# Weights fetched in pairs of blocks, and one partition a unit for the block numbers, in a sparse attention with a channel mix

## The chip, the core and the metric

The kernel runs on one core of a Trainium2 chip. The metric is the device time of one execution in microseconds (us), the median of several. TensorE (PE in the rows) does the matmuls, with its weight loads shown as PEld; VectorE is DVE, ScalarE ACT, GpSimd POOL, and SyncE (SP) issues every DMA transfer of this kernel.

## The reference

Block-sparse attention over 4 sequences of 768 positions, 8 heads of 64, in blocks of 32; then a channel mix on its output, with shifted input, a gate and a squared ReLU.

```python
scores = 0.125 * q @ k.T                      # (4, 8, 768, 768)
mask = |blk_i - blk_j| <= 1 or blk_i, blk_j in (0, 23)
for qb in range(24):                          # three sampled blocks a row of blocks
    for kb in sampled_blocks[qb]:
        mask[qb, kb] = True
x = softmax(where(mask, scores, -1e9)) @ v    # (4, 768, 512)

x_prev = x shifted by one position
xk = mu_k * x + (1 - mu_k) * x_prev
xr = mu_r * x + (1 - mu_r) * x_prev
kk = relu(xk @ w_k) ** 2                      # 512 -> 1024
out = sigmoid(xr @ w_r) * (kk @ w_v)          # 1024 -> 512
```

The three weights w_r (512 x 512), w_k (512 x 1024) and w_v (1024 x 512) arrive as 64-bit floats, everything else as 32-bit floats or integers. The sampled blocks are an input, known only when the kernel runs.

## The kernel before

**Attention** goes by 26 units. A near unit (22 of them, one for each row of blocks n = 1 to 22) takes row n of all four sequences at once: 128 query rows against eight blocks of keys: 0, 23, n-1, n, n+1 and the three sampled ones. Four wide units do rows 0 and 23 of one sequence against all keys. A unit runs through scores (TensorE, line 584), maximum (VectorE, 594), exponentials (ScalarE, 557 or 631), a turn so that the keys lie on partitions (for the first three units by TensorE and a copy, 547 to 553; later by VectorE's transpose, 635, and four transfers, 643), values (TensorE, 617 or 655), division (VectorE, 737 to 748), and a turn of the result into channels by positions (776 and 793, or 757 to 766). Keys go to `KA`, values to `VA`. The neighbours lie in rings of places that the units share; the sampled blocks are fetched by transfers whose source is a register (506 and 523). `keys_again` copies a block that stands in two places.

**The registers** come from `packed`: for each near unit one integer of six 5-bit block numbers (three for keys, and three for values, where a block that is already in the window gets the number of an empty block). `mask_setup` fetches the sampled numbers with the seven numbers that each is compared to (`drawn`, line 334) and packs them by nine VectorE instructions on one partition, 22 units side by side. SP then loads one register a unit (439).

**The weights** are 20 blocks of 128 x 512: four of w_r, eight of w_k, eight of w_v. Each arrives as raw 64-bit words, 0.5 MB in one transfer (425), and is turned into a 32-bit float by a magnitude (ScalarE, 381), a tail (VectorE, 388), a sign (VectorE, 391, or ScalarE, 400, by the set `SIGN_ACT`) and a join (VectorE, 394), and then into two parts that TensorE multiplies fast: the high part (GpSimd, 410, or ScalarE, 412, by `HI_POOL`) and what is left (415; VectorE or GpSimd by `LO_DVE`). The two parts are written to the place of the raw words, which have the same tag `w{i}` and one buffer. The intermediate tiles have three buffers a tag (`zr`, `kk`).

**The channel mix** goes by 12 tiles of 256 positions, tile 1 first and tiles 0 and 11 last: split input (845 to 857), gate for each half (881), hidden part in four pairs of 128 channels (899), values (928), each matmul three times over the parts.

**The order** of all this is made when the kernel is built. Every operation is added to a `Plan` with its engine, a duration, what it reads and writes, and a rank (roughly the time at which it is wanted, lower first), to which a table `SHIFT` adds a number by the operation's position in the list. `Plan.order` runs through time: on each engine, among the operations that could start within `NEAR` ns of the earliest one, it takes that of the lowest rank. A transfer needs one of `FLIGHT` = 8 places in flight, a group of three gathers needs three. It also models that TensorE's instructions come in chunks (`CHUNK` instructions, at least `FETCHED` ns from one to the next). The instructions are then written out in that order, so every engine does its own list strictly in turn, and SP too: a transfer that waits holds up those behind it. The constants (`PICK`, `UNIT_AT`, `RAW_AT`, `WEIGHT_AT`, `SHIFT` and others) stand in the file as numbers.

## Time and profile before

| | |
|---|---|
| median of 3 runs | 536.41 us (532.74, 536.41, 538.78) |
| the profiled execution | 536.71 us |
| its span, first to last instruction | 534.9 us |
| mean granted clock of TensorE | 0.993 of full speed |
| busy: PE, DVE, ACT, POOL | 484.0, 284.9, 327.2, 206.6 us |
| moved by DMA | 115.68 MB, 216 GB/s on the mean |

The profile shows one execution, and its durations are from that one. Busy times are sums over an engine's instructions; issuing transfers doesn't count. A row gives a start in us, a duration, the engine, the line, the operation, out<-in with shapes, a count, and in brackets how long the engine had stood idle and what ended that.

### The profile page before, as it was taken

How to read it: one execution, taken by the hardware profiler on the slowest of the kernel's cores; microseconds unless marked ns; L12 is line 12 of the kernel's file. 1: busy time of each engine (PE TensorE's matmuls, PEld its weight loads, DVE VectorE, ACT ScalarE, POOL GpSimd, SP SyncE). 2: the span in 40 equal slices, each digit the busy share in tenths (PEclk: the TensorE clock that was granted, in tenths of full speed). 3: DMA queues.
4: the chain of work that ended last, by engine and by line, in shares of the span. 5: the costliest groups of instructions: out<-in, count | busy, mean ns of one | idle time of the engine just before them, and what ended most of it. 6: DMA issues, size and time to landing. Idle time of an engine off the chain costs nothing.

```text
span 534.9 us, 17726 instructions
## 1 busy us (share of the span) xinstructions
PE 484.0 (90%) x7260; PEld 394.7 (74%) x7260; DVE 284.9 (53%) x573; ACT 327.2 (61%) x744; POOL 206.6 (39%) x198
## 2 busy tenths in 40 slices
PE   0077699999999999999989999999999999999997
PEld 0034469778768878777967877978877888889896
DVE  2889786765565565465555566375555352223201
ACT  2489986865675676655676566663684662646340
POOL 2354236422612531532621441632351633628270
PEclk9979999999999999999999999999999999999999
DMA  8999988898888888788978897999748433010001
GB/s 303 399 402 326 339 258 245 276 266 263 231 243 257 246 254 245 209 234 225 249 234 255 242 252 235 305 283 335 217 111 290 112 85 81 21 40 1 21 21 39
DMA packets 58628, 115.68 MB, mean 216 GB/s; under 512 B 7730, under 2 KB 20786, under 8 KB 55603
## 3 DMA queue, kind: packets, MB, share of 16 engines
q1 hardware_dynamic: 58546, 114.55, 70.3%
q8 instruction: 57, 0.93, 0.8%
q14 instruction: 25, 0.20, 0.1%
HBM read 77.82 MB, written 6.29 MB: 157 GB/s over the span
## 4 chain that ended last, share of the span: by engine, by line
PE 59%; DMA 16%; SPq 11%; ACT 6%; DVE 4%; issue 4%; POOL 0%; ACTq 0%; DVEq 0%
PE v L928 17%; PE h_3p L899 6%; DMA pt<-r 6%; PE h_0p L899 5%; PE h_2p L899 5%; PE h_1p L899 5%; PE r_1p L881 4%; PE r_0p L881 4%; PE o L655 4%; SPq L643 3%; PE s L584 3%; DMA raw<-w_v 3%; DMA xm<-rx 3%; PE o L719 2%; PE sw L677 2%
## 5 line engine op out<-in xcount | busy, mean ns | idle before, releaser
L928 PE MATMUL v<-w,k 128*128 128x512 f32 (+1 forms) x600 | 143.4, 390 | 0.9 <-ACT h_3k L912 0.9
L928 PEld LDWEIGHTS v<-w,k 128*128 128x128 f32 x600 | 107.2, 188 | 28.8 <-issue 4.9
L584 PE MATMUL s<-KA,q 64*32 64x256 f32 x1408 | 48.5, 399 | 29.4 <-DMA raw<-w_v 25.8
L631 ACT ACTIVATE p<-s,nm 128x256 f32<-128x256 f32 x152 | 63.1, 480 | 8.5 <-DVE r L635 8.3
L635 DVE STREAM_TRANSPOSE r<-p 128x1024 f32<-128x1024 f32 x38 | 45.9, 1228 | 27.1 <-DMA pt<-r 25.9
L584 PEld LDWEIGHTS s<-KA,q 64*32 64x32 f32 x1408 | 25.7, 110 | 44.5 <-issue 34.8
L594 DVE TENSOR_REDUCE nm<-s 128x4 f32<-128x1024 f32 x44 | 53.0, 1213 | 9.6 <-PE s L584 9.3
L655 PEld LDWEIGHTS o<-VA,pt 128*32 128x32 f32 x2432 | 37.1, 109 | 14.7 <-issue 8.2
L655 PE MATMUL o<-VA,pt 128*32 128x65 f32 x2432 | 42.3, 221 | 6.2 <-DMA pt<-r 3.1
L857 POOL TENSOR_TENSOR xr<-xr_0f,xr 128x256 fp32r<-128x256 f32 x24 | 18.4, 765 | 76.2 <-ACT xr L855 67.4
L857 POOL TENSOR_TENSOR xr<-xr_1f,xr 128x256 fp32r<-128x256 f32 x24 | 17.8, 744 | 76.5 <-ACT xr L855 73.8
L899 PEld LDWEIGHTS h_0p<-xk,w 128*128 128x128 f32 x288 | 35.8, 191 | 3.1 <-ACT z L888 1.7
L899 PE MATMUL h_0p<-xk,w 128*128 128x256 f32 x288 | 37.3, 284 | 0.9 <-ACT z L888 0.7
L899 PE MATMUL h_3p<-xk,w 128*128 128x256 f32 x288 | 38.0, 285 | 0.0
L748 DVE TENSOR_TENSOR x<-o,R 128x128 f32<-128x128 f32 x96 | 23.9, 317 | 25.7 <-ACT xt L766 13.6
L899 PEld LDWEIGHTS h_2p<-xk,w 128*128 128x128 f32 x288 | 35.9, 191 | 2.2 <-ACT k L913 0.4
L899 PE MATMUL h_2p<-xk,w 128*128 128x256 f32 x288 | 37.4, 284 | 0.0
L899 PE MATMUL h_1p<-xk,w 128*128 128x256 f32 x288 | 37.2, 284 | 0.0
L899 PEld LDWEIGHTS h_3p<-xk,w 128*128 128x128 f32 x288 | 36.0, 191 | 1.6 <-ACT k L913 0.6
L899 PEld LDWEIGHTS h_1p<-xk,w 128*128 128x128 f32 x288 | 35.6, 191 | 1.3 <-ACT xr_1d L845 0.4
L881 PE MATMUL r_1p<-w,xr 128*128 128x512 f32 x144 | 36.4, 397 | 0.0
L881 PE MATMUL r_0p<-w,xr 128*128 128x512 f32 x144 | 36.4, 397 | 0.0
(139 smaller groups left out, 795.5 us busy)
## 6 DMA issues: line engine op xcount, KB each, us to landing
VA<-vt SPq DMA_DIRECT2D x92, 260.0 KB, 4.2
KA<-kt SPq DMA_DIRECT2D x89, 256.0 KB, 4.4
pt<-r SPq DMA_DIRECT2D x76, 256.0 KB, 5.0
VA<-vw SPq DMA_DIRECT2D x24, 260.0 KB, 4.6
KA<-kq SPq DMA_DIRECT2D x16, 384.0 KB, 5.4
ptw<-rw SPq DMA_DIRECT2D x32, 192.0 KB, 3.9
out<-z SPq DMA_DIRECT2D x23, 256.0 KB, 4.4
q<-qt SPq DMA_DIRECT2D x22, 256.0 KB, 4.7
```

The source lines that it names most:

```text
L584: nc.tensor.matmul(s.ap[ROWS[j], row, a * 256 : (a + 1) * 256].rearrange("p (n x) -> p n x", x=BLK), q.ap[half, (hp * QB + j) * BLK : (hp ...
L594: nc.vector.tensor_reduce(out=nm.ap.rearrange("p (r a) -> p r a", r=2), in_=s.ap.rearrange("p r (a x) -> p r a x", a=2), axis=AX.X, op=ALU ...
L631: plan.add(ACT, 365, t1 + O_EXP[kind], lambda row=row, a=a, i=i: nc.scalar.activation(p.ap[:, :, :, i, :].rearrange("p j c x -> p c j x"), ...
L635: plan.add(DVE, N_TURN, t1 + O_TURN[0], lambda: nc.vector.transpose(out=r.ap[:, :, gi].rearrange("p j c i x -> p j (c i x)"), in_=p.ap.rea ...
L643: nc.sync.dma_start(pt.ap[:, b].rearrange("p g c i x -> p (g c i x)"), r.ap[ROWS[b]].rearrange("p j g c i x -> p j (g c i x)"))
L655: nc.tensor.matmul(o[gi].ap[ROWS[j], i * DV : (i + 1) * DV], pt.ap[:, j, gi, g, 2 * row + a, :], VA.ap[:, c0 + g, j, h * DV : (h + 1) * DV ...
L677: nc.tensor.matmul(s.ap[HALF[a], row, 0:W], q.ap[half, 2 * hp * BLK : 2 * (hp + 1) * BLK], wide_keys(b, hp)[half, k * W : (k + 1) * W], st ...
L748: nc.vector.tensor_tensor(out=to[:, :, 2 * e : 2 * e + 2], in0=o[i].ap.rearrange("p (c e v) -> p c e v", e=2, v=DV)[:, :, e, 0:D].rearrang ...
L857: plan.add(POOL, 160 + 2.17 * MIX * tw, rank + O_MIX, lambda f=f, cs=cs: nc.gpsimd.tensor_tensor(out=dst.ap[:, 1, cs], in0=f.ap, in1=dst.a ...
L881: nc.tensor.matmul(pr.ap[:, 0:512], xr.ap[:, a, c, :], weight_of["r", c].ap[:, w, :], start=(c == 0 and m == 0), stop=(c == CC - 1 and m = ...
L899: nc.tensor.matmul(ph.ap[:, ff * TT : (ff + 1) * TT], weight_of["k", c, f2 // 2].ap[:, w, f % 4 * P : (f % 4 + 1) * P], xk.ap[:, a, c, :], ...
L928: nc.tensor.matmul(pv.ap[:, 0:width], k2.ap[:, a, f, i * P : (i + 1) * P], weight_of["v", f].ap[:, w, cs], start=(f == 0 and m == 0), stop ...
```

## The change

Raw weights come two blocks at a time: ten transfers of 1 MB into tiles of two blocks, whose place then holds the four parts of both blocks. The transfer counts as one write of both halves, and a place is given back as a whole: a tile of parts can be written when the raw tile in the same place has been read for both blocks. The numbers of the sampled blocks lie on 22 partitions, one for each near unit, and are packed there; the register of unit n is loaded from partition n-1. The two mixing vectors come in one transfer, and their complement is made by one instruction. The sets that choose engines for parts and copies, the constants of the order's model and the whole table of ranks are others; what is computed is the same.

```diff
-    CHUNK, FIRST, FETCHED, FLIGHT = 258, 214, 6200, 8
+    CHUNK, FIRST, FETCHED, FLIGHT = 254.05, 186.0, 4600, 8
...
-    packed = fixed([1, NEARS], I32, "packed")
+    packed = fixed([NEARS, 1], I32, "packed")
...
-        drawn = buf([1, 2, pairs, 2], I32, "x0", 1, "drawn")
-        e = buf([1, NEARS, NRAND, SAME_AS], F32, "x1", 1, "equal")
-        r = buf([1, 6, NEARS, NRAND], F32, "kk", 3, "pickf")
+        drawn = buf([NEARS, 2, NRAND * SAME_AS, 2], I32, "x0", 1, "drawn")
+        e = buf([NEARS, NRAND, SAME_AS], F32, "x1", 1, "equal")
+        r = buf([NEARS, 6, NRAND], F32, "kk", 3, "pickf")
...
-        for w, m in enumerate((mu_k, mu_r)):
-            plan.add(SP, ISSUE, 20, lambda w=w, m=m: nc.sync.dma_start(mk.ap[:, w, :], m), writes=[(mk, w)], size=20000)
-            plan.add(DVE, 150, 25, lambda w=w: nc.vector.tensor_scalar(
-                out=mk.ap[:, 2 + w, :], in0=mk.ap[:, w, :], scalar1=-1.0, scalar2=1.0, op0=ALU.mult, op1=ALU.add),
-                reads=[(mk, w)], writes=[(mk, 2 + w)])
+        plan.add(SP, ISSUE, 20, lambda: nc.sync.dma_start(mk.ap[:, 0:2, :], mu), writes=[(mk, 0, 1)], size=40000)
+        plan.add(DVE, 150, 25, lambda: nc.vector.tensor_scalar(
+            out=mk.ap[:, 2:4, :], in0=mk.ap[:, 0:2, :], scalar1=-1.0, scalar2=1.0, op0=ALU.mult, op1=ALU.add),
+            reads=[(mk, 0, 1)], writes=[(mk, 2), (mk, 3)])
...
-            tile_in = raws[name]
-            raw, here = tile_in.ap, (tile_in,)
+            tile_in, half = raws[name]
+            raw, here = tile_in.ap[:, half], (tile_in, half)
...
-        w = buf([P, 2, 512], F32R, f"w{i}", 1, f"w{i}")
-        weight_of[name] = w
+        two = i // 2
+        if i % 2 == 0:
+            pairs[two] = buf([P, 2, 2, 512], F32R, f"w{two}", 1, f"w{two}")
+        whole, e = pairs[two], i % 2
+
+        weight_of[name] = (whole, e)
...
+    def two_blocks(which, c, f=0):
+        w = {"r": w_r, "k": w_k, "v": w_v}[which]
+        return w[c * P : (c + 2) * P, f * 512 : (f + 1) * 512].rearrange("(a p) x -> p a x", p=P)
...
-            for i, (name, src) in enumerate(jobs):
-                raw = raws[name] = buf([P, 512, 2], I32, f"w{i}", 1, f"raw{i}")
-                plan.add(SP, ISSUE, RAW_AT[i], lambda raw=raw, src=src: nc.sync.dma_start(raw.ap.rearrange("p x b -> p (x b)"), src.bitcast(I32)),
-                         writes=[(raw,)], release=RAW_AT[i], size=524288)
+            for i in range(0, len(jobs), 2):
+                name, src = jobs[i]
+                raw = buf([P, 2, 512, 2], I32, f"w{i // 2}", 1, f"raw{i // 2}")
+                for e in range(2):
+                    raws[jobs[i + e][0]] = (raw, e)
+                src = two_blocks(*name)
+                plan.add(SP, ISSUE, RAW_AT[i // 2], lambda raw=raw, src=src: nc.sync.dma_start(raw.ap.rearrange("p a x b -> p a (x b)"), src.bitcast(I32)),
+                         writes=[(raw, 0, 1)], release=RAW_AT[i // 2], size=1048576)
...
-            sampled[n, by] = by.value_load(packed.ap[0:1, n - 1 : n], min_val=0, max_val=ROOM ** (2 * NRAND) - 1)
+            sampled[n, by] = by.value_load(packed.ap[n - 1 : n, 0:1], min_val=0, max_val=ROOM ** (2 * NRAND) - 1)
...
-ISSUE, FETCH, FIND = 560, 760, 850
+ISSUE, FETCH, FIND = 560, 740, 380
...
-HI_POOL = frozenset([0, 1, 7, 9, 10, 16, 17, 18])
-LO_DVE = frozenset([0, 3, 5, 6, 8, 14, 16, 19])
-SIGN_ACT = frozenset([0, 3, 4, 5, 6, 8, 15, 16, 17, 19])
-TURN_DVE = frozenset(['0_1_0', '1_0_1', '1_1_0', '1_1_1', '2_1_0'])
+HI_POOL = frozenset([0, 5, 6, 7, 9, 10, 13, 14, 15, 17])
+LO_DVE = frozenset([5, 6, 8, 16, 18])
+SIGN_ACT = frozenset([0, 1, 4, 5, 6, 15, 16, 19])
+TURN_DVE = frozenset(['0_0_0', '0_0_1', '1_1_0', '1_1_1', '2_0_0', '2_1_0', '2_1_1'])
```

The ranks that SP goes by at the start, each the sum of the operation's constant and its number in `SHIFT`, lowest first, without those whose place is still in use by unit 0. In raw transfers r, k and v are the weight, the digits its row blocks, and f0 and f1 the halves of w_k's columns; q0 is unit 0's q.

| before | rank | after | rank |
|---|---|---|---|
| raw r3 | -5033.9 | drawn | -5284.4 |
| values 0 | -4932.3 | keys 23 | -5270.5 |
| raw v2 | -4912.3 | keys 0 | -4775.0 |
| raw k1 f1 | -4805.7 | raw r2, r3 | -3950.6 |
| raw k2 f0 | -4805.6 | raw v0, v1 | -2008.8 |
| keys 23 | -4769.8 | raw r0, r1 | -957.1 |
| drawn | -4769.6 | raw k2, k3 f0 | -317.2 |
| raw v1 | -4762.9 | raw v6, v7 | -11.8 |
| raw r0 | -4762.8 | q0 | -0.6 |
| values 2 | -4723.9 | keys 1, 2 | -0.3 |
| raw k3 f0 | -4715.7 | q1 | 1.2 |
| q1 | -4514.2 | values 0 | 5.4 |
| sampled keys, unit 0 | -4514.1 | raw v2, v3 | 5.7 |
| raw k1 f0 | -4411.6 | raw k0, k1 f0 | 8.0 |
| mu_k | -177.2 | values 23, unit 1 | 8.1 |
| keys 1, 2 | -175.4 | sampled keys, unit 0 | 8.9 |
| keys 0 | -175.4 | values 1 | 9.7 |
| values 1 | -175.4 | values 2 | 12.9 |
| raw v4 | -131.9 | raw v4, v5 | 19.0 |
| q0 | 11.4 | sampled values, unit 1 | 26.1 |
| raw v0 | 11.5 | values 23 | 29.5 |
| raw r1 | 11.6 | sampled keys, unit 1 | 30.0 |

## Rows read from the trace of the kernel before

**Rows 1.** The page's first line.
```profile
span 534.9 us, 17726 instructions
```
**Rows 2.** Stages (from:to, length): busy us of each engine, TensorE's clock, DMA share, GB/s.
```profile
core 0: us, PE busy (x) PEld busy (x) DVE busy (x) ACT busy (x) POOL busy (x), PEclk, DMA share, GB/s
0.00:26.00 26.00, 0.15 (x8) 0.18 (x16) 13.67 (x28) 8.41 (x13) 7.26 (x13) 1.00 0.93 348
26.00:68.00 42.00, 30.24 (x733) 19.11 (x728) 35.72 (x73) 37.50 (x83) 17.84 (x16) 0.92 0.98 356
68.00:400.00 332.00, 322.02 (x5277) 261.71 (x5276) 193.28 (x391) 217.45 (x506) 124.35 (x116) 1.00 0.85 247
```
**Rows 3.** TensorE's waits, 25 to 70 us: total us, times, longest.
```profile
PE s L584 <- DMA raw<-w_v: 25.8, 1, 25.8
PE t L547 <- ACT p L557: 3.4, 4, 1.8
```
**Rows 4.** TensorE in order of time, 25 to 110 us.
```profile
25.85 3.67 PE L584 MATMUL s<-KA,q 64*32 64x256 f32 x64 [25.85 <-DMA raw<-w_v]
...
62.44 1.67 PE L617 MATMUL o<-VA,pt 128*32 128x65 f32 x99 [0.95 <-issue]
64.41 1.09 PE L584 MATMUL s<-KA,q 64*32 64x256 f32 x28 [0.30 <-ACT nm L598]
66.72 0.62 PE L584 MATMUL s<-KA,q 64*32 64x256 f32 x4 [1.22 <-issue]
...
67.70 3.01 PE L881 MATMUL r_0p<-w,xr 128*128 128x512 f32 x12
```
**Rows 5.** SP's issues in order of time, from the start.
```profile
0.75 0.39 SPq L425 DMA_DIRECT2D raw<-w_r  x1
...
8.38 0.33 SPq L425 DMA_DIRECT2D raw<-w_k  x1
...
16.60 2.14 SPq L508 DMA_DIRECT2D KA<-kt  x3
```
**Rows 6.** Transfers issued up to 18.8 us: count, KB each, us to landing.
```profile
raw<-w_k SPq DMA_DIRECT2D x4, 512.0 KB, 7.2
raw<-w_v SPq DMA_DIRECT2D x3, 512.0 KB, 7.8
KA<-kt SPq DMA_DIRECT2D x5, 256.0 KB, 7.8
raw<-w_r SPq DMA_DIRECT2D x2, 512.0 KB
VA<-vt SPq DMA_DIRECT2D x3, 260.0 KB, 8.2
q<-qt SPq DMA_DIRECT2D x2, 256.0 KB
KA<-kt SPq DMA_DIRECT2D x1, 512.0 KB, 8.1
```
**Rows 7.** Groups by line, 26 to 68 us: busy us, mean ns | idle before.
```profile
L415 POOL TENSOR_TENSOR w<-wf,w 128x512 fp32r<-128x512 f32 x10 | 13.8, 1393 | 8.0 <-ACT w L412 7.2 <-DMA VA<-vt 0.4
L381 ACT ACTIVATE wmag<-raw 128x512 f32<-128x512 f32 x12 | 8.3, 702 | 3.1 <-DMA raw<-w_r 3.1
L388 DVE TENSOR_SCALAR wf<-raw 128x512 uint16<-128x512 uint16 x11 | 5.5, 516 | 0.0
L400 ACT ACTIVATE wf<-raw 128x512 f16<-128x512 f32 x6 | 4.7, 813 | 0.9 <-DMA raw<-w_v 0.9
L412 ACT CAST w<-wf 128x512 fp32r<-128x512 f32 x7 | 4.3, 629 | 0.3 <-DVE wf L394 0.3
```
**Rows 8.** Stages at the start, as in the second group.
```profile
0.00:13.00 13.00, 0.00 (x0) 0.00 (x0) 3.21 (x10) 2.92 (x4) 3.20 (x9) 1.00 0.84 299
13.00:27.00 14.00, 1.15 (x24) 0.76 (x32) 11.28 (x20) 5.49 (x9) 5.06 (x5) 1.00 1.03 400
```
**Rows 9.** VectorE's first packing instruction, in order of time.
```profile
10.01 0.63 DVE L341 TENSOR_TENSOR equal<-drawn 1x462 f32<-1x462 int32 x1 [4.93 <-DMA drawn<-blocks]
```
**Rows 10.** The page's list of transfers.
```profile
KA<-kt SPq DMA_DIRECT2D x89, 256.0 KB, 4.4
```

108 lines of the change are left out of this document (56 added, 52 removed).

## The prediction

> **What bounds the kernel now.** I read the cores' page first for the span, then the busy times of five stages, then what TensorE waited for, and then the start in order of time. The span is 534.9 us [rows 1]; the profiled execution took 536.71 us, so 1.8 us lie around it, and the median of the three runs is 536.41. The sum below is made against 536.7. A difference under 1% (5.4 us) is about what a measurement of this kernel cannot tell from none: its three runs alone lie 6 us apart.
>
> The stages [rows 2] tell where TensorE is not working: 25.9 us of the first 26, 11.8 of the next 42 (42 less 30.24), 10.0 of the 332 up to 400. So from about 68 us TensorE sets the pace with little to win; most of its idle time lies ahead of that. There is one long wait, 25.8 us before the first scores [rows 3]; the view names a weight transfer as its releaser, but the weights are not read by the scores. What they read is q and the keys, the sampled ones last: these were asked for from 16.60 us on, in 2.14 us [rows 5], and took 7.8 us to land [rows 6], which gives 26.5 us, near enough to the start at 25.85 [rows 4]. The first gate starts at 67.70 [rows 4] and with it the mixer, which fills TensorE. Between 26 and 68 us it is ScalarE (37.5 of 42 us) and VectorE (35.7) that are nearly full, and the DMA engines (0.98) [rows 2]. Of ScalarE's 37.5 us, 17.3 are turning raw weights into pairs of parts: 8.3 + 4.7 + 4.3 us [rows 7]. The same engines were busy for only 8.4 and 13.7 us of the first 26 [rows 2]. The start is thus a queue of transfers, and behind it a queue of conversions that stand in the way of the first three units' attention.
>
> **The change, part by part.**
>
> *Transfers.* Nine raw transfers of 0.524 MB were issued before 18.8 us, with six of keys (1.84 MB), three of values (0.80) and one q that is in time (0.26; the second was issued last): 7.62 MB up to the sampled keys [rows 6]. The engines moved 299 GB/s in the first 13 us (3.89 MB) and 400 after [rows 8], so 7.62 MB are through at 13 + 3.73/0.4 = 22.3 us; the first scores come 3.5 us behind that, which I take as the time to land and be seen. In the changed kernel I set the table of ranks in the section on the change against the rule that SP takes the lowest rank among what can start (in the trace of before its first eleven issues, from 0.75 to 8.38 us [rows 5], stand in that order, but for a value transfer whose place was being cleared). Ahead of unit 0's sampled keys then stand seven raw transfers of 1.049 MB (7.34 MB), keys 0 and 23 (0.52), keys 1 and 2 (0.52), two q (0.52), two values (0.53) and the sampled keys themselves (0.79): 10.2 MB, through at 13 + 6.3/0.4 = 28.8 us, so scores at 32.3 us, 6.5 later than now. From below this is bounded by 25.85 (the gathers could go at once when the packed words are there, as they did before), from above by two more values and the eighth raw transfer going first (1.6 MB, 3.9 us: 36.3), since a group of three gathers needs three free places in flight and may lose its turn to single transfers. I take 32.3, the ranks' own order. With larger transfers in flight the first 13 us may also fill better: between 400 and 299 GB/s there are 3.3 us, of which about 2 are the time before the first bytes. I take 1.1 us, with 0 and 1.3 as ends.
>
> *Conversions.* What lands early instead are weights. By 26 us six blocks had their magnitude made (the other lines of that instruction: twelve from 26 to 68 [rows 7], two later); by the order above about eleven have. Five blocks more move into a stretch in which ScalarE had 17.6 us free. One block costs ScalarE 0.70 us for the magnitude, 0.8 x 8/20 for the sign and 0.63 x 10/20 for the high part by the new sets: 1.33 us; five are 6.7 us [rows 7]. The new sets take two signs, two high parts and two turned copies (at some 0.6 us, as a high part) from ScalarE, 4.1 us in all, of which I count 2.5 in this stage. They go to GpSimd and VectorE: GpSimd gets two copies and three subtractions more (3 x 1.39 and less [rows 7]); it is busy 17.8 of these 42 us [rows 2], so this is covered, and if not, a weight comes some 5 us later. ScalarE then has 37.5 - 6.7 - 2.5 = 28.3 us of work, which at today's density (37.5 of 42) lasts 31.7 us. First scores at 32.3 - 1.1 = 31.2, first gate at 62.9 instead of 67.7: **4.8 us gained**, as the difference of a loss of 5.4 and a gain of 10.2.
>
> *Sharing one place by two blocks.* The high part of a pair's first block cannot be written before the raw words of both have been read: that is one magnitude, one tail and one sign more, 0.70 + 0.50 + 0.79 = 2.0 us [rows 7] on one block in two. It costs nothing where weights are early; the queue behind it is GpSimd's or ScalarE's own next copy. If the pair is the one for which the first gate waits, it costs 2.0. Between 0 and 2.0 I take 0, because with this order the gate's blocks land among the first three pairs, some 40 us ahead.
>
> *Fewer issues.* Ten raw issues and one vector's less are some 0.35 to 0.6 us each on SP, 4 to 5 us, in a stretch where SP mostly waits for places in flight. I take 0, with 1 us gained as the other end.
>
> *Packing.* The blocks' numbers landed at 10.0 us, as the wait of the first packing instruction shows [rows 9]; now they go first. Packing on 22 partitions shortens the long instructions: the first, over 462 elements, took 0.63 us [rows 9] and is now over 21. This saves 1 to 2 us of VectorE and makes the gathers ready some 7 us sooner, which by itself gives nothing while they stand behind seven weights. The mixing vectors come in one transfer and take one small instruction of VectorE less, where nobody waits for them: 0. Reading a register from another partition than the first is not in this trace: between 0 and 0.3 us each for 22 of them, off TensorE's path; I take 0.
>
> *The order anew, and its fetch model.* All of the order is worked out again with other constants. One can be read from the trace: after a gap TensorE ran 99 + 28 = 127 matmuls, each with its load (254 instructions), and stood again with no releaser until 66.72, which is 4.3 us after 62.44 [rows 4]. The changed constants say 254 instructions and 4.6 us, the old ones 258 and 6.2. An order that knows this can put such gaps where TensorE waits anyway. The gaps seen here are 0.95 and 1.22 us; I take 1.4 us gained, with 0 and 3 as ends, and for the rest of the span (10.0 us of idle time from 68 to 400) 0, between 4 lost and 4 gained.
>
> **Sum:** 536.7 - 4.8 - 1.4 = **530.5 us**. Put together the ends give 521 to 541.
>
> **Rivals.**
>
> *Scores late, chain as long (slower).* The interval from first scores to first gate was 67.70 - 25.85 = 41.85 us [rows 4]. Three units are a chain (scores, maximum, exponentials, turns, values, division, turn, mixing), and if its latency, not ScalarE's load, sets those 42 us, then the scores that come 6.5 us later push the gate to 74.2 and the time to 543.2. It decides from an interval of 35.3 us: above it the change loses, below it wins. For it speaks that TensorE's own waits in this stage are on steps of the chain (3.4 us for the exponentials [rows 3]); against it that ScalarE is 89% full there, nearly half of it with weights.
>
> *It comes out even.* Gathers are issued as soon as they can be and weights fill in as now, or the interval shrinks by about those 6.5 us only: scores 26 to 32, gate 66 to 68. 536 us, between 533 and 539. For it speaks that the same 10.5 MB of weights and the same keys must pass the DMA engines at 0.98 before the gate.
>
> *Each transfer has a fixed price.* 256 KB land in 4.4 us over the whole run [rows 10] and 512 KB in 7.2 [rows 6]; a straight line through these leaves 1.6 us at no bytes. Were that time of the DMA engines, eleven transfers less would give 17.6 us: 519 us. Against it: with 512 KB transfers the engines already ran at 1.03 busy and 400 GB/s from 13 to 27 us [rows 8], so the 1.6 us overlap with other transfers. The Trainium skill has such a rule ("DMA: Bandwidth & Descriptors", Bandwidth: transfers of 1 MiB or more for 75% of peak, and under Anatomy of one DMA a fixed 2.0 us); as an estimate by that page ten transfers would be 20 us. By that rule half the size should run well below peak; the 400 GB/s in the trace do not bear it out.
>
> *The change does not do what it says*, or the new order has a stall that its model lacks: 528 to 546.
>
> **How the numbers follow.** Forecast 0.58 (522 to 535), even 0.18, slower chain 0.13 (540 to 546), fixed price 0.04, not as said 0.07. The range of 521 to 541 leaves out most of the slower chain, the fixed price and some tails, about 2 in 10; the forecast's own is 522 to 535. Faster by over 1% (under 531.3): some three in five of the forecast's cases, the fixed price and half of the last, 0.44; within 1%: the others of the forecast and the even ones, 0.41; slower (over 542.1): the chain and the rest, 0.15.
>
> **What would show it.** Right: first scores at 30 to 33 us, seven raw transfers ahead of them, ScalarE busier than 13 us in the first 26, first gate at 61 to 64, then TensorE idle as little as now. Wrong: the first gate at 67 or later with late scores (chain); scores at 26 (the order is not as I read it); sampled keys landing well over 8 us after issue; or a gain or loss that arises behind 100 us, of which this argument knows nothing.

## The result, and the profile after

The changed kernel takes 543.56 us (median of 13 runs, 539.03 to 546.35), the kernel before 536.41 (13 runs beside them, 531.55 to 540.09): a ratio of 1.0149, 95% interval 1.0121 to 1.0177. It is 1.5% slower. (Ratios and their intervals, here and below, are taken from the runs within 1.5% of the fastest of the same kernel, so they are not the quotients of the medians beside them.) 530.5 with a range of 521 to 541 was predicted; the sign was wrong too. The rival "scores late, chain as long" had said 543.2.

The profiled execution of the changed kernel took 539.56 us, 4 us under its median, so its span is only 2.5 us over that of before [rows 1]; I come back to this.

```profile
span 537.4 us, 17710 instructions
```

Stages, with the columns of [rows 2]:

```profile
0.00:26.00 26.00, 0.00 (x0) 0.00 (x0) 12.82 (x28) 10.30 (x17) 13.15 (x18) 1.00 0.93 350
26.00:68.00 42.00, 26.79 (x704) 18.27 (x712) 33.92 (x63) 31.43 (x69) 14.26 (x13) 1.00 0.96 346
68.00:400.00 332.00, 321.77 (x5202) 261.72 (x5194) 198.39 (x393) 218.03 (x509) 126.67 (x119) 0.99 0.84 246
```

TensorE does 3.5 us less in the second stage than before (26.79 against 30.24) and the same in the long one. ScalarE is no longer full there: 31.43 us of 42, where it had 37.50. There is less work on the engine that was taken for the limit, and yet TensorE got less done.

SP's issues in order of time (start, length), to be held against [rows 5], and then the transfers issued up to 19 us (count, KB each, median us to landing), against [rows 6]:

```profile
0.75 0.44 SPq L333 DMA_DIRECT2D drawn<-blocks  x1
...
4.14 1.62 SPq L435 DMA_DIRECT2D raw<-w_v  x1
...
21.95 1.76 SPq L518 DMA_DIRECT2D KA<-kt  x3
...
36.82 2.13 SPq L535 DMA_DIRECT2D VA<-vt  x3
```
```profile
raw<-w_v SPq DMA_DIRECT2D x3, 1024.0 KB, 13.7
raw<-w_r SPq DMA_DIRECT2D x2, 1024.0 KB, 8.9
raw<-w_k SPq DMA_DIRECT2D x2, 1024.0 KB, 13.3
KA<-kt SPq DMA_DIRECT2D x1, 512.0 KB, 15.1
```

Seven raw transfers (3 + 2 + 2) stand ahead of unit 0's sampled keys, which go out at 21.95 in place of 16.60. A raw transfer now takes 8.9 to 13.7 us to land, where one of half the size took 7.2 to 7.8; 512 KB of keys behind them took 15.1, before 8.1.

TensorE in order of time (start, length, count; in brackets the idle time before it and what ended it), against [rows 4]:

```profile
31.85 3.67 PE L594 MATMUL s<-KA,q 64*32 64x256 f32 x64 [31.85 <-DMA KA<-kt]
...
48.45 0.99 PE L627 MATMUL o<-VA,pt 128*32 128x65 f32 x52 [2.01 <-issue]
...
70.92 2.48 PE L594 MATMUL s<-KA,q 64*32 64x256 f32 x34 [1.98 <-issue]
...
74.23 4.73 PE L366 MATMUL warm<-const-bfloat16-1.0 128*128 128x512 bf16 x19
78.61 1.74 PE L899 MATMUL r_0p<-w,xr 128*128 128x512 f32 x6
```

First scores at 31.85, 6.0 us later than before. First gate at 78.61, 10.9 later, but 4.4 of that are the warm-up matmuls (74.23 to 78.61), which now stand ahead of the gate and stood behind it in the kernel before (71.67 there, 4.55 us for 20). Without that swap the gate is 6.5 us late against this execution of before; another kernel with the same lists up to its gate (b_nowarm, below) has the gate at 69.37, and against that it is 4.9 us late. The releaser "issue" in these rows means that the profile names nothing that TensorE waited for; I take such stops for waits for its own instructions, as the prediction did from the 254 between two of them, but nothing in the trace names that.

The stretch from scores to gate, in one row for the kernel before and one for the changed one:

```profile
25.85:67.70 41.85, 30.09 (x733) 18.98 (x733) 35.57 (x73) 37.20 (x82) 18.00 (x16) 0.92 0.98 356
```
```profile
31.85:78.61 46.76, 35.37 (x783) 22.64 (x785) 40.43 (x81) 36.74 (x85) 12.68 (x13) 0.96 0.92 308
```

TensorE's idle time in it is 11.8 us before (41.85 less 30.09) and 11.4 after. Its own work is 30 us before and, without the warm-up, 31 after.

**Where the time is in the whole span.** The span is 110 us, plus what TensorE has still to do at 110, plus its idle time behind. By 110 us it had worked 71.74 us before and 66.44 after:

```profile
0.00:110.00 110.00, 71.74 (x1454) 51.34 (x1454) 80.56 (x162) 77.70 (x170) 44.43 (x46) 0.97 0.94 318
```
```profile
0.00:110.00 110.00, 66.44 (x1369) 48.63 (x1371) 76.89 (x151) 71.65 (x158) 46.97 (x50) 0.98 0.90 307
```

Of a total of 484.0 and 482.8 us (the page's busy time) 412.3 and 416.4 were left, and the idle time behind 110 was 12.6 and 11.0. So the start cost 5.3 us against the profiled execution of before, and this execution won back 1.2 in TensorE's busy time and 1.6 in idle time. A second profiled execution of the same kernel (below) lost 8.3 at the start and won nothing back.

### The profile page after: what moved, and what is told of

Its sections match the earlier page's. It is cut to its first block, busy times and chain, and to the rows that moved or that the text cites. A ratio compares the mean times of both kernels' runs of the same rounds, so it can differ in the third digit from the quotient of the medians.

```text
span 537.4 us, 17710 instructions
## 1 busy us (share of the span) xinstructions
PE 482.8 (90%) x7259; PEld 395.6 (74%) x7260; DVE 293.8 (55%) x573; ACT 325.7 (61%) x740; POOL 210.5 (39%) x203
## 4 chain that ended last, share of the span: by engine, by line
PE 58%; DMA 17%; SPq 7%; ACT 7%; DVE 6%; issue 3%; POOL 1%; ACTq 0%; DVEq 0%
PE v L946 17%; DMA pt<-r 6%; DMA raw<-w_v 6%; PE r_1p L899 5%; PE r_0p L899 5%; PE h_1p L917 4%; PE h_2p L917 4%; PE h_3p L917 4%; PE h_0p L917 4%; PE o L665 4%; PE s L594 3%; SPq L653 3%; PE sw L687 2%; PE o L729 2%; DMA xm<-rx 2%
## 5 line engine op out<-in xcount | busy, mean ns | idle before, releaser
L665 PEld LDWEIGHTS o<-VA,pt 128*32 128x32 f32 x2432 | 36.2, 109 | 10.5 <-issue 3.8
L665 PE MATMUL o<-VA,pt 128*32 128x65 f32 x2432 | 40.3, 221 | 4.0 <-DMA VA<-vt 2.4
L917 PE MATMUL h_1p<-xk,w 128*128 128x256 f32 x288 | 38.4, 285 | 0.9 <-ACT h_0k L930 0.9
L858 DVE SCALAR_TENSOR_TENSOR xr_1f<-xt,mk,xr_1d 128x128 f32<-128x128 f32 x48 | 19.7, 410 | 35.6 <-POOL xr L867 30.2
```

Of the source, the lines that this page charges most:

```text
L665: nc.tensor.matmul(o[gi].ap[ROWS[j], i * DV : (i + 1) * DV], pt.ap[:, j, gi, g, 2 * row + a, :], VA.ap[:, c0 + g, j, h * DV : (h + 1) * DV ...
L858: nc.vector.scalar_tensor_tensor(out=parts(f.ap[:, i, :]), in0=cols(c, 1), scalar=mk.ap[:, 2 + which, c : c + 1], in1=parts(d.ap), op0=ALU ...
L917: nc.tensor.matmul(ph.ap[:, ff * TT : (ff + 1) * TT], part_of("k", c, f2 // 2)[:, w, f % 4 * P : (f % 4 + 1) * P], xk.ap[:, a, c, :], star ...
```

## The experiments

The kernels' names begin with a_ where the changed kernel is edited and b_ where it is the one before; n_ and p_ have an order worked out anew. The theories: **O**, the raw transfers ahead of unit 0's sampled keys make the start late, and that is never made up. **S**, the size of a transfer costs. **Q**, conversions that stand ahead of unit 0's steps in ScalarE's and VectorE's lists hold it up. **P**, the shared places cost. **W**, the warm-up ahead of the gate costs. Later **L**, the interval follows the conversions' load, as the prediction had it, and **T**, it is set by waits. Each median stands beside runs of the kernel before on the same chip.

**The late start alone: b_late and b_half.** In SP's list of the kernel before, raw transfers are put ahead of unit 0's sampled keys; nothing else is touched.

```diff
+    late = [924, 913, 931, 922, 916]   # b_half: [924, 913]
+    ahead = [o for o in placed if o.seq in late]
+    placed = [o for o in placed if o.seq not in late]
+    at = next(i for i, o in enumerate(placed) if o.seq == 15)
+    placed[at:at] = ahead
```

> The kernel before with one move in SP's list alone: five raw transfers (2.6 MB) that follow unit 0's sampled keys are put ahead of them. Nothing else of the change is in it. Theory O: first scores 6.5 us later, at 32.4 us, and the time 5 to 7.5 us up, 541 to 544 us. Rival (slack: the weights that come earlier let the conversions run ahead, so the late scores are made up before the first gate): 535 to 538 us.

> The kernel before, with only two raw transfers (one w_r, one w_v, 1.05 MB in all) moved in SP's list ahead of unit 0's sampled keys, where b_late moved five (2.62 MB, scores 5.4 us later, gate 7.7 us later, time 6.7 us longer). If the start is passed on whole (theory O): 1.05 MB at the 400 GB/s of this stage are 2.6 us, so first scores at 28.0 to 28.5 us, first gate at 70 to 71, time 538 to 539.5 (ratio 1.004 to 1.007). If only a step beyond some point counts (the rival in which slack ahead of the gate takes up the first few us): gate within 1 us of 67.7 and the time as before.

```profile
31.25 3.30 PE L584 MATMUL s<-KA,q 64*32 64x256 f32 x64 [31.25 <-DMA VA<-vt]
...
75.38 3.01 PE L881 MATMUL r_0p<-w,xr 128*128 128x512 f32 x12
```
```profile
27.20 3.21 PE L584 MATMUL s<-KA,q 64*32 64x256 f32 x64 [27.20 <-DMA q<-qt]
...
71.02 3.01 PE L881 MATMUL r_0p<-w,xr 128*128 128x512 f32 x12
```

b_late: scores 5.4 us later, gate 7.7 later, 542.86 us, ratio 1.0151 (1.0098 to 1.0204). That is the changed kernel's whole loss without any other part of the change. b_half: scores 1.35 later (I had expected 2.2 to 2.7), gate 3.3 later, 538.79 us, ratio 1.0061 (1.0027 to 1.0094), 3.3 us.

In both the gate is later by 2 us more than the scores. That is a matter of the execution of before that they are held against, not of the delay. b_nowarm (below) has the lists of before up to its gate, and there the gate comes 1.7 us later than in before, though the scores are earlier:

```profile
25.47 3.67 PE L582 MATMUL s<-KA,q 64*32 64x256 f32 x64 [25.47 <-DMA raw<-w_v]
...
69.37 3.01 PE L879 MATMUL r_0p<-w,xr 128*128 128x512 f32 x12
```

The last 14 us ahead of the gate of before, in before and then in b_nowarm:

```profile
54.00:68.00 14.00, 10.09 (x260) 7.17 (x261) 11.21 (x28) 13.46 (x35) 3.27 (x3) 1.00 0.97 335
```
```profile
54.00:68.00 14.00, 12.09 (x255) 7.87 (x255) 10.14 (x24) 11.72 (x32) 2.02 (x2) 0.76 0.71 251
```

About as many matmuls took TensorE 2 us more. Its granted clock was 0.50, the lower of its two levels (1.2 and 2.4 GHz), from 55 to 61 us, behind a stop of 2.04 us, where before had 1.00. b_half (0.50 from 58 to 64) and b_late (0.53 from 61 to 67) have the same stretch, moved with their start. Against b_nowarm, b_half's scores are 1.73 us late and its gate 1.65, b_late's 5.78 and 6.01: up to the gate the delay is passed on one for one, and there is no slack that takes up the first microseconds. That it reaches the end the times show, less sharply: 6.7 us by the medians for b_late and its runs of before, 3.3 by the ratio for b_half with an interval of 1.4 to 5.0. b_half's profiled execution does not show its part (535.39 us, 3.4 under the median; 70.98 us of TensorE's work done by 110, 0.8 less than before), b_late's does (66.63, 5.1 less). O stands.

**The other parts.** a_20x keeps all of the changed kernel but issues each pair as two transfers of 0.5 MB; a_20p also gives each block a place of its own; b_pack takes into the kernel before only the packing on 22 partitions and the one transfer of the mixing vectors; a_nowarm and b_nowarm leave out the warm-up matmuls, which feed no result.

```diff
-  nc.sync.dma_start(raw.ap.rearrange("p a x b -> p a (x b)"), src.bitcast(I32))
+  for e in range(2):                                      # a_20x
+      nc.sync.dma_start(raw.ap[:, e].rearrange("p x b -> p (x b)"), src[:, e].bitcast(I32))
-  raw = buf([P, 2, 512, 2], I32, f"w{i // 2}", 1, f"raw{i // 2}")
+  raw = [buf([P, 512, 2], I32, f"w{i + e}", 1, f"raw{i + e}") for e in range(2)]   # a_20p
-  for i in range(times):
-      nc.tensor.matmul(w.ap, one[:, 0:P], one, start=(i == 0), stop=(i == times - 1))
+  pass                                                    # a_nowarm, b_nowarm
```

> The changed kernel with each 1 MB raw transfer issued as two of 0.5 MB one right behind the other, places and order as they are. Theory O (order: seven raw pairs ahead of unit 0's sampled keys make the first scores 6 us late, and nothing behind makes that up): first scores stay at 31 to 33 us and the time at 541 to 546 us. Theory S (size: what costs is that a 1 MB transfer lands as a whole, later than 0.5 MB, 10.0 against 7.2 us): back to 535 to 539 us.

> The changed kernel, its instruction lists in the same order, with twenty places of one block each and each raw pair as two transfers of 0.5 MB. Theory O: the time stays at 541 to 546 us, the first scores at 31 to 33. Theory P (places: a high part that waits for the raw words of both blocks holds up conversions in the first 60 us, and the attention behind them): 536 to 540 us, with ScalarE and VectorE busier before 40 us than in the changed kernel.

> The kernel before, its instruction lists in the same order, with two parts of the change alone: block numbers packed on 22 partitions, with the registers loaded from them, and one transfer and one instruction for both mixing vectors. Theory O: packing is not what the gathers wait for in SP's list, so the first scores stay at 25 to 26.5 us and the time at 534 to 538 us. Rival (register loads from other partitions are slow, or the vectors' shared transfer is late): 538 to 541 us. Rival (packing sooner lets the gathers go sooner): 533 to 535 us.

> The changed kernel without the matmuls of line 366, which compute nothing that is used; there they stand right ahead of the first gate for 4.5 us. Theory W (the new order costs by this place: they delay the gate): 539 to 541 us. Theory O: the gate comes 4 us earlier, but the attention that the mixer then overlaps is as late as before, 541 to 545 us. Rival (TensorE's clock is kept up by them): a lower granted clock after 74 us, 543 to 547 us.

> The kernel before without the same matmuls (line 368), which there stand behind the first gate, where TensorE next waits for turned exponentials. All theories: 535 to 538 us; if the clock is kept up by them, a lower granted clock after 72 us and 537 to 540 us.

a_20x: 540.82 us, 1.0138 (1.0062 to 1.0215), scores at 32.43, gate at 79.47; the median lies between what O (541 to 546) and S (535 to 539) had said, but the scores are as late as in the changed kernel and the ratio is clear of 1, as O says. a_20p: 542.19, 1.0101 (1.0019 to 1.0183), scores 32.56, gate 79.67. b_pack: 535.59, 0.998 (0.9933 to 1.0028), scores 24.96, gate 69.91. The size, the places and the packing are not the main cause; of the places up to some 2 us stay unclear. Without the warm-up:

```profile
32.43 3.67 PE L592 MATMUL s<-KA,q 64*32 64x256 f32 x64 [32.43 <-DMA KA<-kt]
...
74.50 1.63 PE L897 MATMUL r_0p<-w,xr 128*128 128x512 f32 x6
```

The gate of a_nowarm comes at 74.50, 42.07 us behind its scores, where before had 41.85. That the two are so near is in part chance: the lists of before give 41.85 to 44.95 (table below), and a_nowarm has 32 matmuls of scores more ahead of its gate (764 for 733). The time is 540.52, 1.0113 (1.0056 to 1.017), in the range of W (539 to 541) and just under that of O (541 to 545); b_nowarm 536.18, 0.9999 (0.9962 to 1.0035). Where the warm-up stands moves the gate by 4.4 us and the time by 3 us or less, which these runs do not settle. The third theory of these two, that the warm-up keeps TensorE's clock up, finds little: without it the granted clock was 0.67 from 80 to 84 us in a_nowarm and 0.72 in b_nowarm, but the changed kernel, which has it, had 0.67 from 72 to 76. The low stretch moves, and neither time rises.

**Does the interval follow the load? b_tiny, a_tiny, a_gone.** The step on which the forecast rested. Seven blocks that are converted between scores and gate have their magnitude, tail, sign and joining over 8 columns in place of 512; the instructions, their waits and the transfers stay. a_gone also leaves out two raw transfers behind unit 0's sampled keys, with the waits for them.

```diff
+    LEFT = frozenset([8, 9, 10, 11, 12, 13, 18])   # b_tiny: [1, 2, 4, 10, 12, 17, 19]
+    to = 8 if i in LEFT else 512
-    mag.ap, raw[:, :, 1].bitcast(F32), AF.Copy, scale=2.0**-111)
+    mag.ap[:, 0:to], raw[:, 0:to, 1].bitcast(F32), AF.Copy, scale=2.0**-111)
...
+    lambda raw=raw, src=src, i=i: i in GONE or nc.sync.dma_start(   # a_gone: GONE = 8 to 11
```

> The same cut of load in the kernel before (blocks 1, 2, 4, 10, 12, 17 and 19 over 8 columns in place of 512, three of them with their sign on ScalarE): ScalarE loses 5.3 of its 37.5 us between 26 and 68, VectorE 6 to 8 of 35.7; instructions, waits and transfers stay (most of these weights' values are left out, so the output is not the reference's). Theory L: interval 41.85 x 32.2/37.5 = 36 us, first gate at 61 to 63 in place of 67.7, time 530 to 532. Theory T: gate at 66 to 68.5, time 534.5 to 537.

> The changed kernel, with seven of the blocks that are converted between the first scores and the first gate (8 to 13 and 18) worked on over 8 columns in place of 512 in their magnitude, tail, sign and joining; the high and low parts are filled from these 8 columns, so that all instructions, their waits and the transfers stay, and only the load of ScalarE and VectorE falls (this leaves out most of these seven weights' values, so the output is not the reference's). In the trace of the changed kernel a magnitude is 0.68 us, a tail 0.45, a sign 0.59, a joining 0.75; at some 0.2 us for a small one, ScalarE loses 3.4 of its 31.4 us between 26 and 68 and VectorE 8 of 33.9. Theory L (the prediction's step: the interval follows the load): 46.8 x 28/31.4 = 41.7 us, so the first gate at 73 to 74 in place of 78.6, and the time 4 to 6 us under the changed kernel's (537 to 539). Theory T (the interval is set by waits: transfers in SP's order, fetch gaps and the lists behind them): gate within 2 us of 78.6, time 541 to 544.

> As the run before it, and two of the raw transfers behind unit 0's sampled keys (the pairs of blocks 8 to 11, 2.1 MB, issued at 34.28 and 40.10) left out with the waits for them; these four blocks are a constant (so the output is not the reference's). 2.1 MB are 5.2 us at 400 GB/s. Theory T: unit 0's sampled values and units 1's and 2's keys and q land 2.5 to 5 us earlier, first gate 4 to 6 us earlier than in the run before it; under L nothing changes against that run (within 1 us).

For b_tiny the stretch from its scores to its gate, and the two ends:

```profile
25.06:68.50 43.44, 31.50 (x733) 20.59 (x733) 28.76 (x72) 32.83 (x82) 17.44 (x16) 0.96 0.96 348
```
```profile
25.06 3.67 PE L595 MATMUL s<-KA,q 64*32 64x256 f32 x64 [25.06 <-POOL w L421]
...
68.50 3.01 PE L892 MATMUL r_0p<-w,xr 128*128 128x512 f32 x12
```

ScalarE has 4.4 us less to do (32.83 for 37.20), VectorE 6.8 less (28.76 for 35.57), and the interval is 1.6 us longer; 1.4 of that is TensorE's own busy time, for the same 733 matmuls. The time is 536.55, 1.0001 (0.9962 to 1.004). L (gate at 61 to 63, 530 to 532 us) falls, and with it the prediction's step. What T had said (gate at 66 to 68.5, 534.5 to 537) came. But the relief was not without effect. TensorE's waits, 25 to 70 us, against [rows 3]:

```profile
PE o L628 <- issue: 3.5, 2, 2.4
PE t L558 <- ACT p L568: 1.8, 3, 0.9
...
PE s L595 <- DMA KA<-kt: 1.2, 1, 1.2
PE s L595 <- DMA q<-qt: 1.2, 1, 1.2
```

The waits for the exponentials fell from 3.4 us to 1.8, and others stand in their place: keys and q that had not landed, and stops without a releaser. a_tiny says the same of the changed kernel: VectorE 32.59 us for 40.43, gate at

```profile
78.48 1.71 PE L910 MATMUL r_0p<-w,xr 128*128 128x512 f32 x6
```

and 542.1 us, 1.0109 (1.0068 to 1.0151). a_gone: gate 77.65, 0.8 earlier than a_tiny, not the 4 to 6 that T had expected; 540.98, 1.0077 (1.0039 to 1.0116). So T, with the transfers in SP's order as the waits, came true for b_tiny and a_tiny and falls with a_gone. The table has the interval of all executions whose attention lists up to the gate were not moved against the weights', and of n_pack1 (below). The last column splits TensorE's idle time by what ended it: another engine, a transfer, nothing named.

| kernel | first scores | first gate | interval | TensorE busy in it | idle in it | engine, transfer, nothing named |
|---|---|---|---|---|---|---|
| before | 25.85 | 67.70 | 41.85 | 30.09 | 11.8 | 7.9, 0.2, 3.7 |
| b_nowarm | 25.47 | 69.37 | 43.90 | 32.48 | 11.4 | 8.4, 0.6, 2.2 |
| b_pack | 24.96 | 69.91 | 44.95 | 32.93 | 12.0 | 9.2, 0.5, 2.3 |
| b_tiny | 25.06 | 68.50 | 43.44 | 31.50 | 11.9 | 3.6, 3.3, 5.0 |
| b_half | 27.20 | 71.02 | 43.82 | 32.00 | 11.8 | 9.8, 0, 1.8 |
| b_late | 31.25 | 75.38 | 44.13 | 32.06 | 12.1 | 10.2, 0, 1.8 |
| n_pack1 | 25.49 | 68.32 | 42.83 | 30.77 | 12.1 | 10.7, 0.9, 0.4 |
| a_nowarm | 32.43 | 74.50 | 42.07 | 29.76 | 12.3 | 5.4, 2.0, 4.8 |
| changed | 31.85 | 78.61 | 46.76 | 35.37, 4.4 of it warm-up | 11.4 | 4.9, 1.7, 4.7 |
| changed, again | 33.89 | 80.98 | 47.09 | 35.13, with warm-up | 12.0 | 5.5, 1.9, 4.5 |
| a_20x | 32.43 | 79.47 | 47.04 | 34.20, with warm-up | 12.8 | 5.6, 1.5, 5.5 |
| a_20p | 32.56 | 79.67 | 47.11 | 35.40, with warm-up | 11.7 | 5.6, 2.3, 3.7 |
| a_tiny | 33.36 | 78.48 | 45.12 | 34.59, with warm-up | 10.5 | 3.8, 2.9, 3.8 |
| a_gone | 32.91 | 77.65 | 44.74 | 33.40, with warm-up | 11.3 | 5.5, 3.5, 2.3 |
| a_start | 28.67 | 76.56 | 47.89 | 35.22, with warm-up | 12.7 | 9.8, 0, 2.9 |

The interval is TensorE's own work in a fixed order, 29 to 33 us without the warm-up, and 10.5 to 12.8 us in which it waits. The sum of the waits does not follow the load of the engines beside it, nor when the stretch starts; their make-up does. In b_tiny the waits for other engines fell by 4.3 us (7.9 to 3.6), and those for transfers and with nothing named rose by 4.4 (3.9 to 8.3). In a_tiny, against the changed kernel, the first fell by 1.1 and the others rose by 0.3. Why the sum comes back to about 12 us is not shown by any run.

**Getting the start back by moving things: a_early1, a_early2.** In the changed kernel's lists, a_early1 puts unit 0's sampled keys ahead of two raw transfers, and its last values ahead of another; a_early2 also puts unit 0's attention ahead of the conversions of four blocks.

```diff
+    move([917, 18, 19], 13)    # a raw pair, a value and the sampled values go behind the sampled keys
+    move([912], 52)            # another raw pair goes behind a later key transfer
...
+    part = placed[first:then]  # a_early2
+    placed[first:then] = [o for o in part if not 920 <= o.seq < 1040] + [o for o in part if 920 <= o.seq < 1040]
```

> The changed kernel with four moves in SP's list alone: unit 0's sampled keys go ahead of the raw pairs v2, v3 and k0, k1 (f0), and unit 0's last values ahead of raw v4, v5. Theory O, if the transfers' order alone sets it: first scores 5.2 us earlier (2.1 MB at 0.4 MB per us), at 26.5 us, and the time 4 to 6 us down, 537 to 540 us. Theory Q (the conversions stand ahead of unit 0's maximum in the lists of VectorE and ScalarE): scores at 26.5 us but the maximum still at 34 us, and the time within 2 us of 543.5. Theory S: no change.

> As the one before, and unit 0's maximum, exponentials, turns and copies are put ahead of the conversions of raw blocks v0 to v3 in the lists of VectorE, ScalarE and GpSimd as well. Theory O with Q: the chain of unit 0 runs from 26.5 us on, 6 to 7 us earlier than in the changed kernel, and the time is 536 to 540 us. Rival (load, not latency): the conversions that were put off come back in front of units 1 and 2, and the time stays within 2 us of 543.5.

a_early1, then a_early2:

```profile
26.70 3.57 PE L594 MATMUL s<-KA,q 64*32 64x256 f32 x64 [26.70 <-DMA KA<-kt]
41.38 1.12 PE L557 MATMUL t<-ident,p 128*128 128x128 f32 x4 [11.10 <-ACT p L567]
```
```profile
51.60 2.83 PE L627 MATMUL o<-VA,pt 128*32 128x65 f32 x96 [4.21 <-DVE pt L563]
```

a_early1 has its scores at 26.70, and then TensorE stands 11.10 us for the first exponentials, because conversions stand ahead of them in ScalarE's and VectorE's lists and wait for raw words that now land later. Gate at 84.15, 546.82 us, 1.0198 (1.0111 to 1.0285), outside the ranges of all three theories (Q came nearest). a_early2 has its scores at 28.24, takes that wait away (the exponentials' turn stands at 33.49) and meets others further on, 4.21 us for a copy and 4.19 for unit 1's keys: gate 88.51, 550.48, 1.0281 (1.0213 to 1.0349), above both of its ranges. An early start is worth nothing when the lists behind it are those of a late one. Here the conversions do delay, by their place in a list. TensorE's idle time between scores and gate was 21.5 us in a_early1 and 19.1 in a_early2, where the lists that were not moved have 10.5 to 12.8.

**Other orders: p_early and n_pack1.** p_early has all parts of the change, the engine sets of before and an order of its own that issues only five raw pairs ahead of the sampled keys. n_pack1 is the kernel before with the packing and the vectors' transfer, and an order worked out with the changed constants.

```diff
-    for op in plan.order():
-        op.fn()
+    by_seq = {o.seq: o for o in plan.ops}
+    for seq in ORDER:
+        by_seq[seq].fn()
-    CHUNK, FIRST, FETCHED, FLIGHT = 258, 214, 6200, 8   # n_pack1
+    CHUNK, FIRST, FETCHED, FLIGHT = 254.05, 186.0, 4600, 8   # n_pack1, beside the edits of b_pack
```

> All parts of the change as the changed kernel has them (ten transfers of 1 MB, places shared by two blocks, packing on 22 partitions, one transfer for both mixing vectors), with the sets of engines of the kernel before, and with another order: instruction lists made anew by the kernel's own planner from the ranks of the kernel before, in which five raw pairs, not seven, stand ahead of unit 0's sampled keys. Theory O: first scores at 25 to 27 us, the time back at 534 to 539 us, so that the parts of the change themselves cost under 1%. Rival (the pairs themselves cost, by place or by size, whatever the order): 541 us and more with early scores.

> The kernel before with the packing and the mixing vectors of the change, raw weights still in twenty transfers, and an order made anew from its ranks with the changed constants of the planner. An attempt at a better version: 530 to 538 us. First scores at 25 to 27 us; if they are and the time is over 541 us, the order behind the first gate counts as much as the first scores, against theory O as the only cause.

p_early: 541.05, 1.0107 (1.0044 to 1.0169), with scores at 25.20 and

```profile
35.37 0.69 PE L557 MATMUL t<-ident,p 128*128 128x128 f32 x2 [6.51 <-ACT p L567]
...
40.67 3.73 PE L594 MATMUL s<-KA,q 64*32 64x256 f32 x64 [3.66 <-ACT p L567]
```

the same stand behind conversions, gate at 76.64, 16.5 us idle between scores and gate. O had said 534 to 539, and 541 with early scores is the number of its rival, that the pairs themselves cost. The trace puts the loss on these two stands, and a_20x and a_20p, where pairs are undone, speak against the rival; but no run has this order without the pairs, so it is not ruled out. n_pack1: 542.61, 1.0186 (1.0102 to 1.027), with scores at 25.49, gate at 68.32 and 71.81 us of TensorE's work done by 110, as before. Its loss lies behind that. Of the 4.4 us between the spans (539.3 and 534.9) 2.6 are busy time, which is 486.6 in all, and 1.9 idle time behind 110. From 110 to 200 us, n_pack1 and then before:

```profile
110.00:200.00 90.00, 84.60 (x1401) 69.13 (x1389) 52.14 (x102) 58.12 (x139) 32.26 (x30) 1.00 0.85 246
```
```profile
110.00:200.00 90.00, 86.88 (x1441) 70.68 (x1442) 51.21 (x102) 59.26 (x141) 31.40 (x29) 1.00 0.86 250
```

It does 2.3 us less there and 2.8 less from 300 to 400 (96.31 for 99.07), but between them it gains 3.5, from 200 to 300, n_pack1 and then before:

```profile
200.00:300.00 100.00, 98.21 (x1676) 81.04 (x1683) 62.12 (x127) 63.98 (x156) 34.92 (x34) 1.00 0.87 248
```
```profile
200.00:300.00 100.00, 94.72 (x1564) 78.31 (x1564) 55.21 (x114) 62.36 (x151) 34.34 (x33) 1.00 0.82 235
```

A new order can lose as much as the late start does, though it starts early; O is a way to lose 7 us here, not the only one.

**The early start without moving anything: a_start**, and a second profiled execution of the changed kernel as it is, **a_again**. a_start leaves out two of the seven raw transfers ahead of the sampled keys and the conversions of their four blocks.

```diff
+    GONE = frozenset([4, 5, 14, 15])
+    lambda raw=raw, src=src, i=i: i in GONE or nc.sync.dma_start(...)
...
+    plan.add(DVE, 338, rank, lambda: i in GONE or tail(), ...)
```

> The changed kernel with two of the raw transfers that stand ahead of unit 0's sampled keys left out (the pairs of blocks 4, 5 and 14, 15, 2.1 MB, 5.2 us at 400 GB/s), and with them these four blocks' magnitude, tail, sign and joining; their high and low parts are filled from a constant (so the output is not the reference's). Nothing is moved, and no wait is put ahead of unit 0. If the late start is what costs (the interval of some 47 us from first scores to first gate, warm-up included, stays as it is, because it is TensorE's own 35 us of work and 11 to 12 us of steps it waits for): first scores at 26 to 27.5 us, first gate at 73 to 75, time 5 us under the changed kernel's, 537 to 539.5. If the order behind the start costs by itself: gate as early, but time 541 or more.

> The changed kernel as it is, once more, for a second profiled execution: the first one was 539.6 us, 4 us below the median of its thirteen runs. If the first gate's place is a matter of the order (theory O), it is again at 77.5 to 79.5 us with first scores at 31.5 to 32.5; if those were accidents of one execution, they move by more than 2 us. What the typical execution has on top of the first one should then lie behind 110 us, as idle time of TensorE or as a lower clock. Ratio 1.012 to 1.018.

a_start:

```profile
28.67 3.67 PE L606 MATMUL s<-KA,q 64*32 64x256 f32 x64 [28.67 <-DMA raw<-w_v]
...
66.00 3.33 PE L639 MATMUL o<-VA,pt 128*32 128x65 f32 x128 [2.94 <-DVE wf L398]
...
76.56 1.74 PE L911 MATMUL r_0p<-w,xr 128*128 128x512 f32 x6
```

Scores 3.2 us earlier than in the changed kernel (5 were expected), gate only 2.0 earlier, since TensorE stands 2.94 us behind a conversion at 66. The time is 538.87, 1.0084 (1.0042 to 1.0126), 4.7 us under the changed kernel's by the medians, some 3.5 by the two ratios. The time came out as O says and the gate did not, so this is support and no proof; part of it may be the work left out. a_again: 542.38, 1.0119 (1.0079 to 1.0158); its profiled execution took 547.08, with scores at 33.89 and 63.47 us of TensorE's work done by 110. Neither is where I had expected it (31.5 to 32.5, and a gate at 77.5 to 79.5, where 80.98 came). Against before that is 8.3 us lost at the start, 1.4 more of busy time and 0.4 more of idle time behind: together the 10.1 us between the spans, 545.0 and 534.9. I had expected the execution's extra time behind 110; of the 7.6 us between the two executions of the changed kernel 3.0 lie ahead of it.

## Why the prediction was wrong

*What bounds the kernel.* Right as to the start: the first scores wait for unit 0's sampled keys, and what goes ahead of these on the queue sets when TensorE begins. Wrong as to the stage behind it, below.

*Transfers.* Right in the main. The order read from the ranks, with seven raw transfers ahead, is the order that ran; scores at 32.3 less 1.1 were forecast and 31.85 came. The loss of 5.4 us at this point was there (6.0). The 1.1 us of better filling were not: in the first 13 us the engines moved 293 GB/s, where they had moved 299 [rows 8].

```profile
0.00:13.00 13.00, 0.00 (x0) 0.00 (x0) 4.34 (x15) 3.88 (x6) 4.91 (x11) 1.00 0.82 293
```

*Conversions: the step that failed.* "Five blocks more move into a stretch in which ScalarE had 17.6 us free" and "28.3 us of work, which at today's density lasts 31.7 us", so a gain of 10.2 against the loss. Its first half failed by the landing time. ScalarE's magnitudes in the changed kernel:

```profile
9.01 1.24 ACT L379 ACTIVATE wmag<-raw 128x512 f32<-128x512 f32 x2 [6.77 <-DMA raw<-w_r]
...
14.12 1.23 ACT L379 ACTIVATE wmag<-raw 128x512 f32<-128x512 f32 x2 [1.82 <-DMA raw<-w_r]
...
17.91 1.22 ACT L379 ACTIVATE wmag<-raw 128x512 f32<-128x512 f32 x2
...
25.27 1.78 ACT L379 ACTIVATE wmag<-raw 128x512 f32<-128x512 f32 x3 [3.55 <-DMA raw<-w_v]
```

Six by 25 us, as before, not eleven; ScalarE stood 3.55 us for the next words and was busy 10.30 us by 26, not over 13. Bytes that are asked for early land when the queue has brought them. By the first scores ten were made, four more than before by its first scores, and the second half of the step, that the interval shrinks with ScalarE's load, could show itself: it did not. It is false by itself: b_tiny took 4.4 us from ScalarE and 6.8 from VectorE, and the interval grew by 1.6. The waits for the relieved engines did shrink (by 4.3 us with every engine counted), but waits for transfers and stops with nothing named came in their place (4.4 us), so the interval kept its length and the late start went through to the gate. The trace of before had said so in the row I rested on: TensorE was busy for 30.24 of those 42 us [rows 2]. An interval of 31.7 us would have left it 1.6 us idle in three units' attention, where it was idle for 11.8. I had read the fullest engine as the limit and never set the forecast against the engine whose start and end I was forecasting.

*The rival that came true.* "Scores late, chain as long" named the price: gate at 74.2, time 543.2. Measured: 543.56, and in a_nowarm, where the warm-up does not stand ahead of it, the gate at 74.50. It was to decide from an interval of 35.3 us; the interval was 42 to 45 us where no lists were moved and the warm-up is taken off, with the load gone from it in b_tiny too, and 41 in a_tiny and a_gone. That the time fits to 0.4 us is in part luck, with two executions of the same kernel 7.6 us apart. Its mechanism, the latency of the chain's steps, holds only in part: other engines' steps ended 7.9 of the 11.8 us that TensorE stood in before, and 3.6 of 11.9 in b_tiny. I gave it 0.13, because ScalarE was 89% full; that was no evidence on what TensorE waited for, and the one row that was (3.4 us for the exponentials [rows 3]) spoke for the rival.

*Sharing, issues, packing, vectors at 0.* Borne out within what was measured: b_pack 0.998, a_20p and a_20x like the changed kernel. The packing did become short and early, its first instruction now 0.17 us at 2.32 against 0.63 at 10.01 [rows 9]:

```profile
2.32 0.17 DVE L340 TENSOR_TENSOR equal<-drawn 22x21 f32<-22x21 int32 x1 [2.32 <-DMA drawn<-blocks]
```

and the gathers, ready 17 us ahead, stood behind seven weights, as forecast.

*Fetch gaps, 1.4 us gained.* Not there: 2.01 and 1.98 us with the releaser "issue" ahead of the gate, 4.7 us of such stops in all between scores and gate. Before had 3.7 in all, for beside the 0.95 and 1.22 of [rows 4] there was a third of 1.50 at 53.93, which the prediction passed over.

*A fixed price for each transfer.* Falls: a_20x issues twenty and takes the time of ten, and ten did not come out at 519. The rule weighed there (the Trainium skill, "DMA: Bandwidth & Descriptors", Bandwidth: transfers of at least 1 MiB for 75% of peak) finds no support in these two numbers: 540.82 us with transfers of half the size, 543.56 with the large ones. The fixed 2.0 us that the prediction took from there (the Trainium skill, "DMA: Bandwidth & Descriptors", Anatomy of one DMA) is given for transfers issued by GpSimd. Here SP issues them all, and no run shows that price.

*The sum.* "Put together the ends give 521 to 541" does not follow from the ends that are named: added one by one they give 518.5 to 543.0. The measured 543.56 lies outside both, so the range was too narrow as well, but what put the time there is the step above.

**What stays open.** The places and the position of the warm-up may hold 2 to 3 us of the 7; neither run settles it. And the two profiled executions of the changed kernel lie 7.6 us apart, with 2.0 us between their first scores; why one start is later than the other, no run here tells. Nor does any tell why the stretch at the lower clock falls late in the interval in b_nowarm, b_half and b_late and early in before (granted clock 0.69 from 36 to 42 us). No version that beats the kernel before was found; b_pack equals it.

## What to carry to other kernels

A stretch is as long as the engine at both its ends needs: before saying that it shrinks because a neighbour is relieved, put that engine's own busy time in it beside the forecast, and what it waits for by name. Relieving a neighbour that is 89% full shortens the waits for that neighbour, and the next wait may then show in their place. On one queue, bytes that are needed late, put ahead of those that are needed first, cost these their whole length; here that delay (6.0 us at the first scores) reached the end (7 us by the medians). Where each engine runs a fixed list, moving the transfers without the lists behind them moves the wait, not the work.

## What the runs showed that I had not expected

A longer time to land need not mean a slower transfer. 512 KB of keys took 15.1 us from issue to landing behind raw pairs of 1 MB, 8.1 in before, while the engines' rate to 26 us was the same (350 and 348 GB/s). In a_20x, with the same order in pieces of half the size, the same keys took 10.9 us, but they were issued at 10.86 in place of 6.32 and so landed at about the same time, 21.8 and 21.4. What counted here was the bytes ahead, not the size of the pieces.

TensorE's idle time over three units' attention stayed between 10.5 and 12.8 us in the 15 executions of the table, with starts from 25 to 34 us and quite different loads beside it, while what it waited for changed from one to the next; where lists were moved against each other it was 16.5 to 21.5. And its stops with no releaser come and go with other waits: the one ahead of unit 0's values was 2.01 us in the changed kernel, 2.41 in its second execution, 1.66 in a_tiny, and not there in a_gone.
